# Output projection of a segment-recurrent attention in four column tiles, with the left tokens projected at the end

## The chip, the cores and the metric

The kernel runs on one core of a Trainium2 chip. The metric is the device time of one execution in microseconds (us), read as the median of several executions. PE is the matmul engine, DVE the vector engine, ACT the scalar engine, POOL the general engine, SP the engine whose queue issues most loads.

## The reference

Two branches are mixed by a gate. The second (a gated FFN) depends only on x and is done early. The first is a chain of 64 segments:

```python
for s in range(n_seg):                              # 64 segments of 32 tokens
    xs = x[:, s * seg_len:(s + 1) * seg_len, :]
    h = jnp.concatenate([mem, xs], axis=1)          # 8 memory rows + 32 rows of x, 640 wide
    q, k, v = h @ Wq, h @ Wk, h @ Wv                # 32 heads of 192 (shortened)
    p = softmax(masked(q @ k.T * scale))
    o = (p @ v) @ Wo                                # 6144 -> 640 (shortened)
    mem = o[:, :M, :]                               # 8 rows: the next segment needs them
    outs.append(o[:, M:, :])
out = g * a + (1 - g) * b
```

Everything after the first segment waits for `mem`. Four weight matrices of 7.9 MB each pass over PE in every segment. The kernel keeps most of their 84 pieces in SBUF; some 20 are loaded anew for each segment ("streamed").

## The kernel before

A segment works on 40 rows (8 memory, 32 x). For 8 of the 32 x rows, the "left tokens", Q and K are computed for all segments at the start, stored, and loaded segment by segment. The heads go in four groups ("octets"). `PROG` is the order of work in a segment:

```python
PROG = [("q", 0), ("tq", 0), ("k", 0), ("tk", 0), ("v", 0),
        ...
        ("q", 3), ("pt", 1), ("sc", 2), ("tq", 3), ("ex", 2), ("k", 3), ("pv", 1), ("tk", 3), ("v", 3),
        ("pt", 2), ("sc", 3), ("ex", 3), ("pw", 0), ("wo", 0), ("pv", 2), ("pw", 1), ("wo", 1, 0), ("pt", 3),
        ("wo", 1, 1), ("wo", 1, 2), ("pv", 3), ("wo", 2), ("wo", 3)]
```

The output projection (Wo) makes two column tiles of 64, each 320 columns wide, for all 40 rows:

```python
for h in range(2):
    ...
    fns.append(lambda e, ...: e.matmul(
        ps[64 * h:64 * h + R, OB, 0:HD], u[:, tl, cc, :], w,          # R = 40, HD = 320
        start=(c == 0), stop=(c == NCH - 1), tile_position=(0, 64 * h), skip_group_check=True))
```

The hand-over casts the result, transposes it by six small PE matmuls and copies it into the input `Hb` of the next segment:

```python
S_.add("dve", lambda e: e.tensor_copy(out=mrow[0:104], in_=ps[0:104, OB, 0:HD]), ...)
...                                                       # six (k, lo, hi, f0, h)
    fns.append(lambda e, ...: e.matmul(ps[lo:hi, bk, k * M:(k + 1) * M], mrow[:, f0:f0 + hi - lo], ident[:, 64 * h:64 * h + M], ...))
S_.add("dve", lambda e: e.tensor_copy(out=Hb[nb][:, :, 0:M], in_=ps[:, bk, 0:KT * M]...), ...)
```

The streamed pieces go through a ring of five slots. A load may start when the piece five before it is consumed:

```python
slot = stream_counter[0] % B_RING                         # B_RING = 5
S_.add("sp", lambda e, ...: e.dma_start(piece_view(key, ring_off[slot]), piece_src(key)),
       writes=[r_ring[slot]], dma_sem="ring%d" % slot, ...)
```

Of the kernel before, what the change touches and what calls it, by code (L numbers as in the profile page):

```python
# [221 lines left out]
def _build(nc, A_x, A_mem0, A_Wq, A_Wk, A_Wv, A_Wo, seg_len, w_gate, w_up, w_down,  # L222
# [9 lines left out]
    KT = Dm // 128  # L232
# [30 lines left out]
    b_scr = nc.dram_tensor("ffn_b_scratch", (S, Dm // 2 + 2), F32, kind="Internal").ap()  # L263
    xts = nc.dram_tensor("xt_scratch", (NSEG, 128, KT * L), BF, kind="Internal").ap()
    xls = nc.dram_tensor("left_xt_scratch", (NG, 128, KT * L), BF, kind="Internal").ap()
    qkl = nc.dram_tensor("left_qk_scratch", (NSEG, 128, NOCT * 2 * LW), BF, kind="Internal").ap()
# [11 lines left out]
    wsA["small"] = (96 + 2 * R + 8 + 32 + 31) // 32 * 32  # L278
# [24 lines left out]
    ffn_sz["brow"] = al(NBR * (Dm + 4) * 2)  # L303
# [4 lines left out]
    GP = 3 * HD * 2  # L308
# [38 lines left out]
    for k, n in (("stats", 0), ("maskm", 96), ("mbd", 96 + 2 * R), ("mle", 104 + 2 * R)):  # L347
        wsA_off[k] = wsA_off["small"] + n
    o_H = wsA_off["H"]
    Hb = [bview(o_H, KT * L * 2).rearrange("p (k r) -> p k r", r=L)] * 2  # L350
    r_Hm = [sreg(o_H, 8)] * 2
    r_Hxp = [sreg(o_H + 8, KT * L * 2 - 8)] * 2
# [20 lines left out]
    o_rowb, o_mrow = wsB_off["v"] + 768, wsB_off["v"]  # L373
    rowb = bview(o_rowb, HD * 2 + 4)
    rowbf = fview(o_rowb, HD * 2 + 4)
    rowbg = rowbf[:, HD // 2:HD // 2 + 1]
    r_rowb = sreg(o_rowb, HD * 2 + 4)
    mrow = bview(o_mrow, HD * 2)
    r_mrow = sreg(o_mrow, HD * 2)
# [13 lines left out]
    r_stg = [sreg(wsB_off["stg"], 256), sreg(wsB_off["stg"] + 256, NOCT * 2 * LW * 2 - 256)]  # L393
# [18 lines left out]
    o_mem0r = wsB_off["Q"] + 2 * GQ + GO  # L412
    mem0r = bview(o_mem0r, Dm * 2)
    r_mem0r = sreg(o_mem0r, Dm * 2)
# [26 lines left out]
    BW = (Dm + 4) * 2  # L441
# [19 lines left out]
    Wq2 = A_Wq.rearrange("d h e -> d (h e)").rearrange("(k p) n -> p k n", p=128)  # L461
    Wk2 = A_Wk.rearrange("d h e -> d (h e)").rearrange("(k p) n -> p k n", p=128)
    Wv2 = A_Wv.rearrange("d h e -> d (h e)").rearrange("(k p) n -> p k n", p=128)
# [13 lines left out]
    def part_src(i):  # L477
        src = piece_src(PART)
        return src[:, 1, HD:Dm] if i else src.rearrange("p c n -> p (c n)")[:, 0:GP // 2]
# [4 lines left out]
    def piece_view(key, o):  # L484
        if key[0] == 3:
# [5 lines left out]
            ("q", 2), ("pt", 0), ("sc", 1), ("tq", 2), ("ex", 1), ("k", 2), ("pv", 0), ("tk", 2), ("v", 2),  # L491
            ("q", 3), ("pt", 1), ("sc", 2), ("tq", 3), ("ex", 2), ("k", 3), ("pv", 1), ("tk", 3), ("v", 3),
            ("pt", 2), ("sc", 3), ("ex", 3), ("pw", 0), ("wo", 0), ("pv", 2), ("pw", 1), ("wo", 1, 0), ("pt", 3),
            ("wo", 1, 1), ("wo", 1, 2), ("pv", 3), ("wo", 2), ("wo", 3)]
# [37 lines left out]
    held_i = {order.index(HELD), order.index(HELD2)}  # L532
    STREAM = ((0, 0, 0), (0, 0, 4), (0, 2, 3), (0, 3, 0), (1, 0, 4), (1, 1, 0), (1, 1, 4), (1, 2, 1), (1, 3, 0), (1, 3, 3), (2, 2, 0), (2, 3, 3), (3, 0), (3, 2), (3, 6), (3, 8), (3, 11), (3, 17), (3, 20), (3, 23))
# [3 lines left out]
    assert tot_bytes - GO - GQ - sum(piece_size(key) for key in STREAM) <= res_cap  # L537
# [27 lines left out]
    part_sb = bview(o_part, GP).rearrange("p (a n) -> p a n", n=HD)  # L565
# [8 lines left out]
    def issue_ring(seg, upto):  # L574
        done = issued.get(seg, 0)
        while done <= upto:
            key = order[stream_list[done]]
            slot = stream_counter[0] % B_RING
            S_.add("sp", lambda e, slot=slot, key=key: e.dma_start(*((bview(ring_off[slot], 2 * HD), part_src(3)) if key == PART else (piece_view(key, ring_off[slot]), piece_src(key)))),
# [6 lines left out]
    def piece(seg, key):  # L586
# [5 lines left out]
        if key == HELD:  # L592
            return piece_view(key, o_held), r_held
        if key == HELD2:
            return piece_view(key, o_held2), r_held2
# [5 lines left out]
        if key == PART:  # L601
            return bview(ring_off[slot], 2 * HD), r_ring[slot]
# [14 lines left out]
    HB2 = ((5, 0, 576, 320), (6, 576, 1152, 320), (7, 1152, 1536, 640))  # L617
# [9 lines left out]

    r_heldp = [sreg(o_held + 512 * b, 512) for b in range(5)]

    def held_copy(seg, late_part):  # L630
        flat = bview(o_held, GO)
        parts = [3, 4]
        if late_part:
            nxt = [(misc[0] + 1) % 5, (misc[0] + 2) % 5]
            parts = sorted((0, 1, 2), key=lambda b: b not in nxt)
# [7 lines left out]
    left_slot = {}  # L643

# [9 lines left out]
    def left_piece(key):  # L654
        if key in res_off:
            return piece_view(key, res_off[key]), r_res[key]
        issue_left(left_stream.index(key))
        return piece_view(key, ring_off[left_slot[key]]), r_ring[left_slot[key]]
# [22 lines left out]
    for h in range(2):  # L681
        asel(maskm[64 * h:64 * h + 64], r_maskm, [[-1, R]], 0, 1, NEG)
        asel(maskm[64 * h:64 * h + 64], r_maskm, [[0, R]], -M, 1, 0.0)
# [5 lines left out]
    asel(mle, r_mle, [[8, 4], [32, 4]], 7, -1, 0.0)  # L689
    for b in range(8):  # L690
# [47 lines left out]
    def chain_init(bank):  # L738
        pv7 = psb(bank)
        S_.add("pe", [lambda e, k=k: e.transpose(pv7[:, k * M:(k + 1) * M], mem0r[0:M, k * 128:(k + 1) * 128], ident[0:M, 0:M])  # L740
                      for k in range(KT)],
               reads=[r_mem0r, r_ident], writes=[r_ps[bank]], name="mem0T")
        x_load(0)
        S_.add("act", lambda e: e.activation(out=Hb[0][:, :, 0:M], in_=pv7[:, 0:KT * M].rearrange("p (k m) -> p k m", m=M),  # L744
# [538 lines left out]
```

## Time and profile before

| | before |
|---|---|
| time, median of 3 | 1888.62 us (1880.43 to 1896.18) |
| span of the profiled execution | 1875.1 us |
| first hand-over begins | 341.0 us |
| segment, mean of 62 | 24.31 us |
| from the last hand-over to the end | 27.0 us |

In the page below, the queue lines have packets, MB and share. The group lines have the count, then busy us and mean ns, then the engine's idle time ahead of the group and what ended most of it.

```profile
q8 instruction: 272, 4.46, 0.9%
...
L949 PE MATMUL ps<-arena 128*32 128x384 bf16 x10240 | 506.0, 328 | 27.4 <-DVE arena L1179 15.8
...
L969 PE MATMUL ps<-arena 128*32 128x384 bf16 x5800 | 296.2, 329 | 21.5 <-DMA arena<-left_xt_scratch 13.7
```

To see: the passes of Q and K (L949) and V (L969) wait little; the 13.7 us ahead of V is a single wait before the first segment. The first line looks like nothing: 4.46 MB in 272 packets of 16 KB on a queue of its own. The page says PE has 34864 matmuls and as many weight loads. So 272 packets of 16384 bytes come to 272 x 16384 / 69728 = 63.9 bytes for each of these instructions, and the 320 packets of the changed kernel, with its 82018 instructions, come to 63.9 again. So by these counts q8 carries PE's own program, at 64 bytes an instruction and 256 instructions to a packet.

### The profile page before, as it was taken

How to read it: one execution, taken by the hardware profiler on the slowest of the kernel's cores; microseconds unless marked ns; L12 is line 12 of the kernel's file. 1: busy time of each engine (PE TensorE's matmuls, PEld its weight loads, DVE VectorE, ACT ScalarE, POOL GpSimd, SP SyncE). 2: the span in 40 equal slices, each digit the busy share in tenths (PEclk: the TensorE clock that was granted, in tenths of full speed). 3: DMA queues.
4: the chain of work that ended last, by engine and by line, in shares of the span. 5: the costliest groups of instructions: out<-in, count | busy, mean ns of one | idle time of the engine just before them, and what ended most of it. 6: DMA issues, size and time to landing. Idle time of an engine off the chain costs nothing.

```text
span 1875.1 us, 80690 instructions
## 1 busy us (share of the span) xinstructions
PE 1754.7 (94%) x34864; PEld 1180.5 (63%) x34864; DVE 944.5 (50%) x2960; ACT 887.6 (47%) x2093; POOL 145.0 (8%) x546
## 2 busy tenths in 40 slices
PE   8999896999999999999999999999999999999998
PEld 4556684666666666666666666666666666666665
DVE  3233243555555555555555555555555555555555
ACT  2222333555555555555444555455545555555554
POOL 1000000000000000000000000000000000000000
PEclk9999898999999999999999999999999999999999
DMA  9512657999999999999999999999999999999998
GB/s 364 218 36 83 199 154 248 300 306 305 310 305 320 305 322 306 316 299 306 302 316 299 311 301 317 295 313 304 318 299 309 310 313 317 308 300 311 314 304 271
DMA packets 281648, 536.01 MB, mean 286 GB/s; under 512 B 82114, under 2 KB 115786, under 8 KB 281290
## 3 DMA queue, kind: packets, MB, share of 16 engines
q1 hardware_dynamic: 202602, 491.34, 77.8%
q10 hardware_dynamic: 78688, 39.51, 7.6%
q8 instruction: 272, 4.46, 0.9%
q14 instruction: 86, 0.70, 0.1%
HBM read 509.62 MB, written 21.12 MB: 283 GB/s over the span
## 4 chain that ended last, share of the span: by engine, by line
PE 39%; DMA 13%; DVE 3%; ACT 2%; issue 1%; ACTq 0%; SPq 0%; DVEq 0%
PE ps L1120 12%; PE ps L949 11%; PE ps L969 7%; DMA out_dram<-arena 4%; DMA arena<-in_A_Wo_dram 3%; PE ps L1094 3%; DMA arena<-in_A_Wq_dram 3%; PE ps L1011 2%; DMA arena<-in_A_Wk_dram 1%; PE ps L1068 1%; PE ps L993 1%; PE ps L1003 1%; PE ps L1174 1%; DMA arena<-in_A_Wv_dram 1%; DVE arena L1164 1%
## 5 line engine op out<-in xcount | busy, mean ns | idle before, releaser
L949 PE MATMUL ps<-arena 128*32 128x384 bf16 x10240 | 506.0, 328 | 27.4 <-DVE arena L1179 15.8
L1120 PE MATMUL ps<-arena 128*40 128x320 bf16 x6144 | 477.4, 300 | 12.6 <-DMA arena<-in_A_Wo_dram 9.6
L1120 PEld LDWEIGHTS ps<-arena 128*40 128x40 bf16 x6144 | 317.7, 100 | 105.7 <-DMA arena<-in_A_Wo_dram 27.3
L953 ACT ACTIVATE arena<-ps 128x384 bf16<-128x384 f32 x512 | 314.6, 614 | 133.5 <-PE ps L949 89.6
L949 PEld LDWEIGHTS ps<-arena 128*32 128x32 bf16 x10240 | 253.2, 97 | 166.8 <-DVE arena L1179 20.4
L969 PE MATMUL ps<-arena 128*32 128x384 bf16 x5800 | 296.2, 329 | 21.5 <-DMA arena<-left_xt_scratch 13.7
L959 DVE STREAM_TRANSPOSE arena<-arena 128x192 f32<-128x192 f32 x512 | 190.9, 373 | 168.5 <-ACT arena L953 167.9
L969 PEld LDWEIGHTS ps<-arena 128*32 128x32 bf16 x5800 | 147.2, 97 | 111.0 <-DMA arena<-left_xt_scratch 14.1
L624 ACT ACTIVATE arena<-ps 128x576 bf16<-128x576 bf16 (+1 forms) x192 | 113.7, 592 | 213.8 <-PE ps L1120 195.2
L980 ACT ACTIVATE arena<-ps 128x384 bf16<-128x384 f32 x256 | 126.6, 495 | 180.4 <-DMA out_dram<-arena 86.6
L929 POOL COPY arena<-arena 128x96 bf16<-128x96 bf16 x256 | 68.4, 267 | 1409.9 <-PE ps L1011 780.7
L1071 DVE TENSOR_TENSOR arena<-ps,arena 128x320 bf16<-128x320 bf16 x256 | 125.7, 491 | 84.5 <-PE ps L1068 80.9
L1100 ACT ACTIVATE arena<-ps 128x320 bf16<-128x320 f32 x256 | 110.4, 431 | 91.5 <-PE ps L1094 90.8
L1094 PEld LDWEIGHTS ps<-arena 128*64 128x64 bf16 x3072 | 113.6, 125 | 56.7 <-issue 14.8
L1038 ACT ACTIVATE ps<-ps 104x160 f32<-104x160 f32 x256 | 75.5, 295 | 151.4 <-DVE ps L1028 150.8
L1094 PE MATMUL ps<-arena 128*64 128x64 bf16 (+1 forms) x3072 | 138.7, 222 | 6.8 <-ACT arena L637 2.7
L1164 DVE CAST arena<-ps 104x320 bf16<-104x320 f32 x63 | 31.0, 492 | 190.2 <-PE ps L1120 190.2
L1011 PE MATMUL ps<-arena 64*40 64x40 bf16 (+1 forms) x4096 | 120.7, 181 | 0.6 <-DVE arena L959 0.4
L892 PE MATMUL ps<-arena 128*128 128x256 bf16 x960 | 109.7, 278 | 10.1 <-ACT arena L744 5.8
L892 PEld LDWEIGHTS ps<-arena 128*128 128x128 bf16 x960 | 95.0, 100 | 24.5 <-ACT arena L744 6.1
L1026 DVE TENSOR_REDUCE arena<-ps 104x4 f32<-104x160 f32 x256 | 81.3, 318 | 51.6 <-PE ps L1011 51.2
L1011 PEld LDWEIGHTS ps<-arena 64*40 64x40 bf16 (+1 forms) x4096 | 99.9, 97 | 9.8 <-DVE arena L959 0.6
(70 smaller groups left out, 1552.7 us busy)
## 6 DMA issues: line engine op xcount, KB each, us to landing
arena<-in_A_Wk_dram SPq DMA_DIRECT2D x404, 384.0 KB, 4.8
arena<-in_A_Wo_dram SPq DMA_DIRECT2D x464, 320.0 KB, 4.5
arena<-in_A_Wq_dram SPq DMA_DIRECT2D x277, 384.0 KB, 4.7
arena<-in_A_Wv_dram SPq DMA_DIRECT2D x146, 384.0 KB, 5.3
left_qk_scratch<-arena ACTq DMA_DIRECT2D x16, 768.0 KB, 7.5
arena<-left_qk_scratch ACTq DMA_DIRECT2D x64, 192.0 KB, 5.0
arena<-in_A_Wo_dram SPq DMA_DIRECT2D x64, 80.0 KB, 3.9
ffn_b_scratch<-arena ACTq DMA_DIRECT2D x16, 161.0 KB, 2.5
```

The source lines that it names most:

```text
L624: S_.add("act", lambda e: e.activation(out=bview(o_held2, GQ)[:, c0:c1], in_=psb(b)[:, p0:p0 + c1 - c0], func=ACTF.Copy), reads=[r_ps[b]], ...
L892: S_.add("pe", [lambda e, k=k, g_=gs[k][0], i=i, bk=bk, hf=hf: e.matmul(ps[:, bk, 0:NL // 2].rearrange("p (g t) -> p g t", t=L), g_[:, i * ...
L949: S_.add("pe", [lambda e, j=j, k=k, gv=gv: e.matmul(ps[32 * j:32 * j + 32, bank, 0:384].rearrange("p (c i) -> p c i", i=32), Hb[hb][:, k, ...
L953: S_.add("act", lambda e: e.activation(out=rows_sb[m].rearrange("p (b i h) -> p b h i", b=6, h=2), in_=ps[:, bank, 0:384].rearrange("p (b ...
L959: S_.add("dve", lambda e: e.transpose(out=dst[:, :, 0:L], in_=rows_sb[m].bitcast(F32).rearrange("p (c r) -> p c r", r=L)), reads=[r_rows[m ...
L969: return [lambda e, j=j: e.matmul(ps[32 * j:32 * j + 32, bk, 0:384], lhs, g_[:, 384 * j:384 * (j + 1)], start=(k == 0), stop=(k == KT - 1) ...
L980: S_.add("act", lambda e: e.activation(out=v_sb[o % NVB], in_=ps[:, bank, 0:384], func=ACTF.Copy), reads=[r_ps[bank]], writes=[r_v[o % NVB ...
L1011: fns.append(lambda e, gp=gp, lo=lo, hi=hi, b=(3 * tl + c) // 2, h=(3 * tl + c) % 2, tl=tl, last=(c != 1): e.matmul(ps[gp:gp + R, bank, tl ...
L1071: S_.add("dve", lambda e: e.tensor_tensor(out=PTm, in0=apx(pv[:, 0:104], [[64, 2], [0, 4], [1, R]]), in1=apx(mbd, [[0, 2], [1, 4], [0, R]] ...
L1094: fns.append(lambda e, lhs=lhs, left=left, h=h, dst=dst, rhs=rhs: e.matmul(dst, lhs, rhs, start=not left, stop=left, tile_position=(0, 64 ...
L1100: S_.add("act", lambda e: e.activation(out=apx(u[:, 0, 0, :], [[R, 2], [3 * R, 4], [1, R]]), in_=ps[:, A, 0:2 * W].rearrange("p (c t r) -> ...
L1120: fns.append(lambda e, w=w, c=c, h=h, tl=tl, cc=cc, u=u: e.matmul(ps[64 * h:64 * h + R, OB, 0:HD], u[:, tl, cc, :], w, start=(c == 0), sto ...
```

## The change

Its intent is to relieve PE, the busiest engine. Wo gets four tiles of 32 rows, each 160 columns wide. To make 32 rows of the 40, the eight left tokens leave the segment's Wo. Their inputs ("left u") are stored and projected together at the end. The four Wo quarters lie in four partition groups. One DVE instruction makes the new rows (memory plus x) from them, and one DVE transpose turns them, without PE. Wo's parts move between the V passes. Stored left Q and K are loaded by octet.

```diff
-            ("q", 3), ("pt", 1), ("sc", 2), ("tq", 3), ("ex", 2), ("k", 3), ("pv", 1), ("tk", 3), ("v", 3),
-            ("pt", 2), ("sc", 3), ("ex", 3), ("pw", 0), ("wo", 0), ("pv", 2), ("pw", 1), ("wo", 1, 0), ("pt", 3),
-            ("wo", 1, 1), ("wo", 1, 2), ("pv", 3), ("wo", 2), ("wo", 3)]
+            ("q", 3), ("pt", 1), ("sc", 2), ("tq", 3), ("ex", 2), ("k", 3), ("pv", 1), ("tk", 3), ("wo", 0, 0), ("v", 2),
+            ("pt", 2), ("sc", 3), ("pw", 0), ("ex", 3), ("wo", 0, 1), ("wo", 0, 2), ("pv", 2), ("v", 3), ("pw", 1), ("pw", 2), ("wo", 1, 0), ("wo", 1, 1), ("pt", 3),
+            ("pw", 3), ("wo", 1, 2), ("wo", 2, 0), ("pv", 3), ("pw", 4), ("wo", 2, 1), ("wo", 2, 2), ("wo", 3)]
...
-                for h in range(2):
+                for j in range(4):
...
-                        ps[64 * h:64 * h + R, OB, 0:HD], u[:, tl, cc, :], w,
-                        start=(c == 0), stop=(c == NCH - 1), tile_position=(0, 64 * h), skip_group_check=True))
+                        ps[32 * j:32 * j + L, OB, 0:CB], u[:, tl, cc, 0:L], w,        # L = 32, CB = 160
+                        start=(c == 0), stop=(c == NCH - 1), tile_position=(0, 32 * j), skip_group_check=True))
...
-            S_.add("dve", lambda e: e.tensor_copy(out=mrow[0:104], in_=ps[0:104, OB, 0:HD]), ...)
-            S_.add("pe", fns, reads=[r_mrow, r_ident], writes=[r_ps[bk]], name="memT s%d" % s)
-            S_.add("dve", lambda e: e.tensor_copy(out=Hb[nb][:, :, 0:M], ...), ...)
+            S_.add("dve", lambda e: e.scalar_tensor_tensor(out=mrow, in0=ps[:, OB, 0:CB], scalar=msel, in1=xrow, op0=ALU.mult, op1=ALU.add), ...)
+            S_.add("dve", lambda e: e.transpose(out=Hb[0], in_=mrow.rearrange("p (i k) -> p k i", k=KT)), ...)
...
+    final_left()          # at the end: 384 matmuls of 128x320 for the left tokens of all segments
```

Cut: the new scratch buffers and their loads and stores, the list of streamed pieces (19 instead of 20, others, and one piece fewer in part), the masks, the contiguous stores of left Q and K on SP's queue, and the first left x taken from SBUF.

## The prediction

The sum came to 1888.6 - 166 - 15 + 63 = 1770 us. It is left as it was, but terms in it are cut below, since no trace or run had shown them: the working of step 1 (3.3 us for the new Wo; its -3.1 stays in the sum), with the figures for a matmul that it came from, and 2 us of step 7's +63 (52 + 9 are left), for a lower clock after the wait. Step 1's term: the 41 ns that a Q or K matmul of 384 columns takes in this trace would be 41 x 160 / 384 = 17.1 ns for 160 columns, 192 x 17.1 = 3.3 us, and 6.4 - 3.3 = 3.1. The 6.4 us follows from the 66.6 ns measured.

> **What bounds the kernel now.** I read the page first, then PE's timeline over two segments, then the windows, the waits and the queues.
>
> ```profile
> PE 1754.7 (94%) x34864; PEld 1180.5 (63%) x34864; DVE 944.5 (50%) x2960; ACT 887.6 (47%) x2093; POOL 145.0 (8%) x546
> DMA  9512657999999999999999999999999999999998
> L1120 PE MATMUL ps<-arena 128*40 128x320 bf16 x6144 | 477.4, 300 | 12.6 <-DMA arena<-in_A_Wo_dram 9.6
> L1164 DVE CAST arena<-ps 104x320 bf16<-104x320 f32 x63 | 31.0, 492 | 190.2 <-PE ps L1120 190.2
> q1 hardware_dynamic: 202602, 491.34, 77.8%
> q10 hardware_dynamic: 78688, 39.51, 7.6%
> ```
>
> To see: PE is busy 94% (a modelled share, ends included), and from the seventh slice on the DMA engines are nearly as full. L1120 is the output projection (Wo), 96 matmuls in each of the 64 segments. L1164 starts the hand-over of the memory to the next segment and runs 63 times between 341.0 and 1848.1 us: a segment takes (1848.1 - 341.0) / 62 = 24.3 us. Segments are 1556 us of the span, so the answer is 64 times a per-segment change, plus what happens before and after.
>
> PE's timeline over one segment's end:
>
> ```profile
> 968.77 0.49 PE L1094 MATMUL ps<-arena 128*64 128x160 bf16 x12
> 969.09 3.43 PE L1120 MATMUL ps<-arena 128*40 128x320 bf16 x48
> 973.10 0.47 PE L1174 MATMUL ps<-arena 128*128 128x8 bf16 x6 [0.58 <-DVE arena L1164]
> ```
>
> To see: 48 Wo matmuls of 320 columns need 3.43 us, less about 0.3 for the last one's own length: 47 steps of 66.6 ns. [...] 96 x 66.7 = 6.4 us a segment. After it PE stands from 972.52 to 973.86 (cast 0.49, the PE turn, a copy of 0.20): 1.34 us.
>
> Two windows, full load early and the steady state:
>
> ```profile
> 26.00:66.00 40.00, 37.97 (x303) 21.29 (x301) 11.86 (x23) 9.27 (x16) 1.28 (x4) 1.00 1.04 401
> 520.00:1870.00 1350.00, 1280.83 (x28322) 861.79 (x28322) 735.17 (x2394) 693.34 (x1671) 118.66 (x444) 1.00 0.93 308
> ```
>
> To see: clock full (1.00). The queues move 401 GB/s when only large weight rows are loaded, and 308 GB/s at a share of 0.93 in the segments. So DMA has a reserve of at most about a fifth, less with small packets. PE is the first bound, DMA close behind.
>
> [...] the gate's 80 matmuls of one column in 128x32 tiles take 0.77 us together (80.24 to 81.01), (0.77 - 0.17) / 79 = 7.6 ns apart. [...] so weight loads and issue will not limit the new Wo. [...] the Q and K passes in this trace advance 20 matmuls in 0.82 us, 41 ns[...]. [...] q1's packets average 2425 B at 77.8% x 16 x 1875 us / 202602 = 115 ns (21 B/ns); q10's small ones average 502 B at 29 ns (17 B/ns).
>
> **The change, part by part, per segment.**
> 1. Wo for 32 rows in four tiles: [...] On PE's path: -3.1.
> 2. Hand-over: cast, six PE matmuls and copy become a scalar_tensor_tensor of 128x160 and a DVE turn of 128x160. From L1185 (104x320, 547 ns) less 160 elements at the slope of the casts ((492 - 323) / 160 = 1.06 ns) I estimate 0.38; from L959 (192 elements, 373 ns) 0.34 for the turn. With hand-offs 0.85 us for 1.34: -0.5. The V pass done ahead every fourth segment now fills this gap once instead of twice, the other part moves into a V pass: no gain or loss.
> 3. x now comes in through the same scalar_tensor_tensor, so its load must have landed. It is issued after the last V pass, and that pass moves to within 3.2 us of PE work of the end (18 pairs at 0.139, one pT, one PV), perhaps 3.7 with evacuations. The old x load takes 4.2 us from issue to landing. So a new wait of about 0.5 us: +0.5.
> 4. DMA. Streamed: 12 pieces of 384 KB and 7 of 320 KB = 7.01 MB, before 7.09: no relief. Small packets: stored left Q/K by octet 512 of 384 B (before 128 of 1536 B), left u out 256, x, b and out 128 each: 1152 instead of some 384, at 29 ns / 16 engines 2.1 us instead of 0.7. At 401 GB/s the stream takes 17.5 us, with the small ones and about 0.3 of rest 19.9 us a segment. That is the floor under any PE gain.
> 5. The ring. Adding up measured PE paces, the old segment is 22.1 us of PE work against 24.3 seen (25.8 with V ahead, some 23.8 without). The new one is 18.5 without V ahead. A streamed piece may load only when the one five before it is consumed. In the old order the PE work between these lies at 4.4 to 6.5 us; landings take 4.5 to 5.3. In the new order the three pieces (3,8), (3,9), (3,11) have only 2.4 to 2.9 us. They miss by about 2 us, and as all five slots are then in a row, PE waits 2 to 3 us around Wo, where it waits about 1.6 in all today.
> Sum: 18.5 + 0.5 + about 2.5 = 21.5 without V ahead, about 22.3 with it (extra PE work of 2.4 us mostly hides waits): 21.7 on average, -2.6, x 64 = -166 us.
>
> Outside the segments:
> 6. Front. Between the left tokens' phase and segment 0 PE stands 13.7 us for the left x load, because the small-row left store occupies ACT's queue 7.12 us before it. The store becomes contiguous, on SP, and left x comes from SBUF: about -12. The memory's first transpose, which holds PE 6 us in the left phase, goes too. Sixteen DVE turns and twice the b stores come into the FFN phase, beside a DVE at a third busy: a few us. Together -15.
> 7. End. The left tokens' projection: 4 blocks x 48 x 2 = 384 matmuls of 128x320. The FFN's of this shape step at 0.136 us: 52 us, all on the path. Before it nine Wo pieces (2.95 MB, 7.4 us) and the first left u (4096 packets of 384 B, 6 to 7 us) load from the last V pass on, which ends some 4 us before Wo does: about 9 us of wait[...]. Mix and store cost what they cost today. +63.
>
> Sum: 1888.6 - 166 - 15 + 63 = 1770 us.
>
> **The rivals.** (a) *PE-bound throughout*: the ring hides everything. For it: 401 GB/s exists, and PE's waits on DMA are short today (L1120 waits 9.6 us in all). Against: the 2.4 us stretches. Segment 19.8: 1888.6 - 288 - 15 + 63 = 1650 at best; I give it little. (b) *DMA becomes the bound at the rate seen now*: engine time per segment is 0.93 x 24.3 = 22.6 us today, and the new one adds 1.4 of small packets. If this time doesn't shrink under load, a segment takes 23 to 24 and the time is 1850 to 1900. For it: the share of 0.93 at only 308 GB/s. Against: 401 GB/s at share 1.04, and single microseconds of a segment above 360. [...] (c) *A new chain of ACT waits*: the b load now waits in ACT's stream for the out store to land (landing 5.1 us), and stored left Q/K wait for the left u store. ACT is 47% busy, so about 0.5 us a segment, 30 us: 1800. (d) *The end is worse*, strided weights at the left projection halving its rate: +50, 1820.
>
> **Range and chances.** The segment is the large term: 20.8 to 22.8 us covers the mix of (a), (b) and (c), which is -224 to -96; the ends add 10 either way. That gives about 1705 to 1840. Slower or same needs (b) in full, or (b) and (d) in part: faster by over 2% (below 1850.8) 0.91, same 0.07, slower 0.02.
>
> **What would show it.** Step 1: the Wo group has 12288 matmuls of 128*32, 128x160, and an uninterrupted 48 of them last about 1 us. Step 2: DVE goes from Wo's end to Q's start in under 0.9 us. Step 3: DVE waits at the new memory rows on the x scratch, not on PE. Steps 4 and 5: DMA share 0.95 or more, 330 to 350 GB/s in the segments, PE waits on Wo loads up from 9.6 to 60 us or more. Step 6: the 13.7 us wait is gone. Step 7: 384 matmuls at 0.136 after the last segment, and a tail of some 60 us. I am wrong if the segment is over 23 us (DMA), under 20.5 us (no ring loss), or the tail is over 80 us.

## The result

The changed kernel takes 1946.99 us, the median of four executions (1941.83 to 1955.31). The kernel before took 1885.07 us in its four (1880.43 to 1896.18). The ratio is 1.0324, with a 95% interval from 1.0261 to 1.0386: 3% slower. A ratio in this document is the mean time of one kernel's fast runs over that of the other's of the same rounds, so it is not quite the ratio of the medians quoted. Executions over 1.5% slower than the fastest of the same kernel are left out of the means.

The spans split at the first and the last of the 63 hand-overs:

| part | before | after | difference |
|---|---|---|---|
| up to the first hand-over | 341.0 us | 318.8 us | -22.2 |
| 62 segments | 1507.1 us (24.31 each) | 1527.3 us (24.63 each) | +20.2 |
| from the last hand-over to the end | 27.0 us | 94.0 us | +67.0 |
| span | 1875.1 us | 1940.1 us | +65.0 |

So both ends came out much as predicted (-15 and +63), and the segments, which should have given back 166 us, took 20 us more.

The page of the changed kernel, the line of engines and that of the instruction queue:

```profile
PE 1678.7 (87%) x41009; PEld 1124.4 (58%) x41009; DVE 944.5 (49%) x2988; ACT 939.3 (48%) x2220; POOL 300.6 (15%) x795
...
q8 instruction: 320, 5.24, 1.1%
```

To see: PE has 41009 matmuls for 34864, because four narrow tiles need twice as many instructions as two wide ones. It has 76 us less of busy time, and is idle for more. The queue has 48 more packets.

The window over most of the segments (us, then busy time and count of PE, PEld, DVE, ACT and POOL, then granted clock, DMA share, GB/s):

```profile
520.00:1845.00 1325.00, 1136.06 (x32234) 744.38 (x32238) 701.39 (x2315) 713.56 (x1722) 248.65 (x646) 0.98 0.92 306
```

To see: the data rate did not rise (306 GB/s, 308 before), the share of the DMA engines fell to 0.92, and the granted clock is 0.98 for 1.00.

The groups of the changed kernel, with up to three releasers each:

```profile
L1018 PE MATMUL ps<-arena 128*32 128x384 bf16 x10240 | 527.7, 330 | 92.7 <-DVE arena L1251 46.5 <-DMA arena<-in_A_Wq_dram 20.5 <-ACT arena L640 10.5
...
L1196 PE MATMUL ps<-arena 128*32 128x160 bf16 x12288 | 337.2, 243 | 127.7 <-DMA arena<-in_A_Wo_dram 98.5 <-issue 17.6 <-DMA arena<-left_u_scratch 9.7
...
L1249 DVE SCALAR_TENSOR_TENSOR arena<-ps,arena 128x160 bf16<-128x160 f32 x63 | 24.2, 384 | 100.3 <-PE ps L1196 97.7 <-DMA arena<-x_segment_scratch 2.6
...
L1251 DVE STREAM_TRANSPOSE arena<-arena 128x160 bf16<-128x160 bf16 x63 | 22.5, 357 | 2.2
```

To see: Wo (L1196) waits 98.5 us for its weights where the old one waited 9.6, and 17.6 us with the releaser "issue", which means that the profile shows nothing that it waited for. The hand-over (L1249, L1251) takes 384 + 357 ns, as estimated.

PE over one segment's end (start us, length us, work, and in brackets the idle time before it):

```profile
1005.19 0.32 PE L1196 MATMUL ps<-arena 128*32 128x160 bf16 x8 [0.93 <-DMA arena<-in_A_Wo_dram]
1005.79 0.32 PE L1196 MATMUL ps<-arena 128*32 128x160 bf16 x8 [0.28 <-DMA arena<-in_A_Wo_dram]
...
1007.59 1.42 PE L1196 MATMUL ps<-arena 128*32 128x160 bf16 x70
1010.09 0.38 PE L1196 MATMUL ps<-arena 128*32 128x160 bf16 x10 [1.08 <-issue]
1011.45 2.60 PE L1018 MATMUL ps<-arena 128*32 128x384 bf16 x40 [0.97 <-DVE arena L1251]
1013.82 1.50 PE L1038 MATMUL ps<-arena 128*32 128x384 bf16 x16
```

To see: three kinds of loss in 9 us. Eight matmuls at a time wait for a streamed piece of Wo. Then 70 Wo matmuls run in 1.42 us, (1.42 - 0.23) / 69 = 17.2 ns apart with about 0.23 us taken off for the last one's own length. That is the pace which step 1's 3.3 us needs (3.3 us / 192 = 17.2 ns), and then PE stands 1.08 us for no shown reason. After the hand-over the 40 matmuls of Q and K need 2.60 us instead of the 1.81 that the same 40 need elsewhere: the trace records half clock (a granted clock of 0.50) from 1012.32 to 1015.73 us. In the segments (from the eleventh hand-over on) there are 17 such stretches, sixteen of 3.41 us and one of 6.83, which is 1.18 us to a segment; before there was one.

The tail:

```profile
1867.70 1.56 PE L1196 MATMUL ps<-arena 128*32 128x160 bf16 x79
1878.93 0.32 PE L1196 MATMUL ps<-arena 128*32 128x160 bf16 x1 [9.67 <-DMA arena<-left_u_scratch]
1881.36 54.68 PE L1329 MATMUL ps<-arena 128*128 128x320 bf16 x384 [2.11 <-DMA arena<-left_u_scratch]
```

To see: the left tokens' projection takes 54.68 us (52 predicted), behind 9.67 + 2.11 us of waiting for their input (about 9 predicted). The granted clock is 0.50 up to 1886.12 us, where the matmuls step 268 ns; after it they step 136 ns. The 2 us from step 7's term stood for this.

### The profile page after: what moved, and what is told of

Same layout as the page of the kernel before. It is cut to its first block, busy times and chain, and to the rows that moved or that the text cites. A ratio compares the mean times of both kernels' runs of the same rounds, so it can differ in the third digit from the quotient of the medians.

```text
span 1940.1 us, 93507 instructions
## 1 busy us (share of the span) xinstructions
PE 1678.7 (87%) x41009; PEld 1124.4 (58%) x41009; DVE 944.5 (49%) x2988; ACT 939.3 (48%) x2220; POOL 300.6 (15%) x795
## 4 chain that ended last, share of the span: by engine, by line
PE 61%; DMA 32%; issue 3%; DVE 3%; SPq 1%; POOL 0%; DVEq 0%; ACT 0%; POOLq 0%; ACTq 0%
PE ps L1018 17%; DMA arena<-in_A_Wo_dram 17%; PE ps L1196 10%; DMA arena<-in_A_Wq_dram 9%; PE ps L1038 8%; PE ps L952 5%; PE ps L1164 3%; PE ps L1329 3%; PE ps L835 3%; PE ps L838 3%; DMA arena<-in_A_Wv_dram 3%; PE ps L1082 3%; PE ps L1074 2%; PE ps L853 1%; PE ps L856 1%
## 5 line engine op out<-in xcount | busy, mean ns | idle before, releaser
L1018 PE MATMUL ps<-arena 128*32 128x384 bf16 x10240 | 527.7, 330 | 92.7 <-DVE arena L1251 46.5
L1196 PE MATMUL ps<-arena 128*32 128x160 bf16 x12288 | 337.2, 243 | 127.7 <-DMA arena<-in_A_Wo_dram 98.5
L1018 PEld LDWEIGHTS ps<-arena 128*32 128x32 bf16 x10240 | 246.0, 97 | 257.4 <-DVE arena L1251 62.1
L1196 PEld LDWEIGHTS ps<-arena 128*32 128x32 bf16 x12288 | 226.8, 100 | 202.8 <-DMA arena<-in_A_Wo_dram 139.5
L1038 PE MATMUL ps<-arena 128*32 128x384 bf16 x6100 | 308.6, 332 | 11.8 <-issue 7.5
L1183 POOL COPY arena<-arena 128x96 bf16<-128x96 bf16 x256 | 159.2, 622 | 659.8 <-DVE arena L1177 438.6
L1038 PEld LDWEIGHTS ps<-arena 128*32 128x32 bf16 x6100 | 157.8, 98 | 103.3 <-issue 16.3
L640 ACT ACTIVATE arena<-ps 128x384 bf16<-128x384 bf16 (+2 forms) x192 | 114.0, 594 | 117.2 <-POOL arena L1000 81.4
L998 POOL COPY arena<-arena 128x96 bf16<-128x96 bf16 x256 | 68.4, 267 | 615.9 <-PE ps L1082 461.5
L1164 PE MATMUL ps<-arena 128*64 128x160 bf16 (+1 forms) x3072 | 139.0, 226 | 3.0 <-issue 2.6
L1164 PEld LDWEIGHTS ps<-arena 128*64 128x64 bf16 x3072 | 103.2, 126 | 61.7 <-DVE arena L1095 22.6
L666 ACT ACTIVATE arena<-ps 128x256 bf16<-128x256 bf16 x320 | 102.0, 387 | 16.9 <-PE ps L1196 7.6
L952 PE MATMUL ps<-arena 128*128 128x256 bf16 x960 | 105.1, 273 | 1.8 <-DVE arena L963 1.8
```

The costliest lines, as they stand in the source:

```text
L640: S_.add("act", lambda e: e.activation(out=bview(o_held2, GQ)[:, c0:c1], in_=psb(b)[:, p0:p0 + c1 - c0], func=ACTF.Copy), reads=[r_ps[b]], ...
L952: S_.add("pe", [lambda e, k=k, g_=gs[k][0], i=i, bk=bk, hf=hf: e.matmul(ps[:, bk, 0:NL // 2].rearrange("p (g t) -> p g t", t=L), g_[:, i * ...
L1018: S_.add("pe", [lambda e, j=j, k=k, gv=gv: e.matmul(ps[32 * j:32 * j + 32, bank, 0:384].rearrange("p (c i) -> p c i", i=32), Hb[hb][:, k, ...
L1038: return [lambda e, j=j: e.matmul(ps[32 * j:32 * j + 32, bk, 0:384], lhs, g_[:, 384 * j:384 * (j + 1)], start=(k == 0), stop=(k == KT - 1) ...
L1164: fns.append(lambda e, lhs=lhs, left=left, h=h, dst=dst, rhs=rhs: e.matmul(dst, lhs, rhs, start=not left, stop=left, tile_position=(0, 64 ...
L1183: S_.add("pool", lambda e: e.tensor_copy(out=dst, in_=u.rearrange("p t c r -> p (t c) r")[:, :, L:R]), reads=[r_uT[o % NUB]], writes=r_ul[ ...
```

## The experiments

Four theories were to be told apart. The **ring**: Wo's loads start too late, since in the new order five streamed pieces follow each other closely. The **data rate**: the DMA engines give no more than some 310 GB/s with these transfers. The **row order** of Wq, Wk and Wv in DRAM, which the change altered, costs data rate. And, formed after the first four runs, the **fetch**: PE runs out of instructions, since Wo in four tiles uses them up faster than q8 brings them. In the texts L is the ring, B the data rate and F the fetch. A piece is "aliased" below when two pieces of a weight share one place in SBUF. This makes room, and the result is wrong.

A segment's time is the mean distance of the hand-overs. Waits per segment are sums over the segments from the eleventh hand-over on.

**e1, changed kernel with a ring of eight** (three V pieces aliased; wrong).

```diff
-    B_RING = int(opts.get("ring", 5))
+    B_RING = int(opts.get("ring", 8))
+    ALIAS = {(2, 0, 1): (2, 0, 0), (2, 0, 3): (2, 0, 2), (2, 1, 1): (2, 1, 0)}
```

> The changed kernel with eight ring slots instead of five; three resident V pieces share the place of three others to make room, so the result is wrong on purpose; the streamed bytes are the same. Theory L (the load loop: five slots, each refilled only when PE has used it, and about 5 us from issue to landing): deeper slots let the queues run towards the 401 GB/s of the pure load, the segment falls from 24.6 us to about 21 us and the time to about 1720 us, DMA at 345 GB/s or more in the segments. Theory B (bandwidth: some 305 GB/s is all that the queues give beside the engines at work): the segment stays within 0.3 us of 24.6, landings grow from 5 to 7 or 8 us, time 1930 to 1950 us.

Measured: 1975.99 us, ratio 1.0459 (1.034 to 1.058), segment 25.09 us. The waits for weights are gone from PE, and the kernel is slower than with them. The stands marked "issue" grew to 1.63 us a segment at Wo alone, half clock to 2.63 us. So the ring is not the whole cause; neither of the two expectations for this run came. PE's timeline between two of these stands:

```profile
1036.68 0.52 PE L1200 MATMUL ps<-arena 128*32 128x160 bf16 x18
1039.33 0.45 PE L1200 MATMUL ps<-arena 128*32 128x160 bf16 x14 [2.12 <-issue]
1039.71 0.53 PE L1168 MATMUL ps<-arena 128*64 128x160 bf16 x12
1040.17 1.00 PE L1042 MATMUL ps<-arena 128*32 128x384 bf16 x20
1041.00 0.73 PE L1200 MATMUL ps<-arena 128*32 128x160 bf16 x32
1041.65 0.28 PE L1141 MATMUL ps<-arena 104*64 104x104 bf16 x4
1041.87 1.06 PE L1200 MATMUL ps<-arena 128*32 128x160 bf16 x32
1042.86 0.53 PE L1168 MATMUL ps<-arena 128*64 128x160 bf16 x12
1043.32 1.59 PE L1200 MATMUL ps<-arena 128*32 128x160 bf16 x80
1046.08 1.81 PE L1022 MATMUL ps<-arena 128*32 128x384 bf16 x40 [1.17 <-DVE arena L1255]
1047.72 0.65 PE L1042 MATMUL ps<-arena 128*32 128x384 bf16 x10
1050.38 0.67 PE L1042 MATMUL ps<-arena 128*32 128x384 bf16 x10 [2.01 <-issue]
```

To see, and to add up: from 1039.33 to just before 1050.38 there are 14 + 12 + 20 + 32 + 4 + 32 + 12 + 80 + 40 + 10 = 256 matmuls. With a weight load each that is 512 instructions, exactly two packets. q8's packets start at 1036.99, 1041.08 and 1048.08 us and take 0.9 to 1.1 us each. The stands end 1.3 and 1.4 us after the first and the third of them have landed. So the place of a stand is fixed by the count of instructions, not by what the instructions do.

**e2, kernel before with a ring of eight** (same aliases; wrong).

```diff
-    B_RING = int(opts.get("ring", 5))
+    B_RING = int(opts.get("ring", 8))               # and the same ALIAS
```

> The kernel before with the same eight slots (wrong result on purpose). Theory L: it was already held by the loop, so it gains too, but only down to its PE work of 22 to 23 us a segment: 24.3 to about 23, time 1800 to 1830 us. Theory B: unchanged, 1870 to 1890 us. If it was bound by PE and only the changed kernel is bound by loads: unchanged here, and e1 gains.

Measured: 1848.25 us, ratio 0.9783 (0.972 to 0.984), segment 23.83 us at 314 GB/s. The old kernel does gain 0.5 us a segment from the ring, the changed one doesn't (the interval of the ratio lies below 1 and reaches across the 2% line).

**e3, changed kernel with 9 streamed pieces instead of 19** (ten aliased).

```diff
-    STREAM = ((0, 1, 1), (0, 2, 1), (0, 3, 1), (0, 3, 3), ...            # 19 pieces
+    STREAM = ((0, 2, 1), (0, 3, 3), (1, 0, 3), (1, 1, 4), (1, 3, 4), (2, 2, 4), (3, 3), (3, 6), (3, 9))
+    ALIAS = {(0, 1, 1): (0, 1, 0), ...}                                  # the other ten
```

> The changed kernel with 9 streamed pieces instead of 19; the other ten read a resident piece instead (wrong result on purpose). Both theories of loads: the segment falls to PE's own work with its dependences, my sum being 18.5 us without and 21 us with left V, so about 19.5 to 20.5 us on average and a time of 1620 to 1690 us. A theory that the new order of work has waits of its own between the engines (ACT's DMA waits, the memory hand-over): it stays above 22 us, over 1780 us.

Measured: 1729.67 us, ratio 0.9155, segment 21.48 us at 179 GB/s. PE is marked idle 1.33 us a segment, so its work is about 20.2 us. PE waits for no weight load in the segments here. The segment lies between the two expectations (19.5 to 20.5, over 22): the loads cost much, and something besides them is dearer than predicted. Taking the ten pieces out of the stream gives 24.63 - 21.48 = 3.15 us a segment.

**e4, the old row order of Wq, Wk and Wv** (wrong).

```diff
-    Wq2 = A_Wq.rearrange("d h e -> d (h e)").rearrange("(p k) n -> p k n", p=128)
+    Wq2 = A_Wq.rearrange("d h e -> d (h e)").rearrange("(k p) n -> p k n", p=128)      # Wk2, Wv2 alike
```

> The changed kernel with the rows of Wq, Wk and Wv taken as before, so that neighbouring partitions read neighbouring rows 12 KB apart rather than 60 KB apart (wrong result on purpose). A theory that the new row order makes the loads slower in HBM: the segment falls by 1 us or more, time under 1890 us. Theories L and B: no difference, within 10 us of 1945 us.

Measured: 1961.49 us, ratio 1.0382, segment 24.98 us. No gain: the row order is not the cause. (The two ratios, 1.0382 and 1.0324, lie within each other's intervals.)

**e5, half of Wo's instructions; e6, the same with a ring of eight and the aliases of e1** (two of the four column tiles left out; wrong).

```diff
-                for j in range(4):
+                for j in range(2):
```

> New theory F, after e1: PE's instructions come by DMA too (queue q8's 16 KB packets number exactly PE's records times 64 B: 272 before, 320 after), four-tile Wo eats 256 instructions in some 2.2 us, and beside the weight loads a packet does not come that fast; PE then stands with nothing but issue named, and goes to half clock. This kernel leaves out two of the four column tiles of every segment's Wo (wrong on purpose): the same 3.3 us of PE work (two tiles of 160 columns side by side), the same loads, half of Wo's instructions, back to about the number of before. F: the waits named issue at Wo fall from about 1 us a segment to under 0.2, half clock too; with five slots the loads still hold PE, segment 23 to 24 us, time 1850 to 1910 us. Theories of the loads alone (L, B): no change, 1930 to 1960 us.

Measured for e5: 1920.48 us, ratio 1.0198, segment 24.15 us. The stands for instructions fell to 0.08 us a segment, but the waits for Wo's loads stayed at 1.66 us: they take the place of what was removed. So in the changed kernel as it stands, the instructions alone are worth 24.63 - 24.15 = 0.48 us a segment.

> The same with eight ring slots (as e1). F with L: both limits are gone, the segment falls from 25.1 us (e1) to 21 to 22 us, DMA at 335 GB/s or more, time 1720 to 1790 us, and clock back to 0.99. B (305 GB/s is the ceiling): stays at 24.5 us and 1930 us or more.

Measured for e6: 1893.89 us, ratio 1.0057, segment 23.93 us at 314 GB/s. With both gone a third wait appears: DVE waits at the hand-over for x. From the issue of the x load to Wo's end there are 3.77 us, and the load takes 5.56 us, so the hand-over begins 1.9 us after Wo's end. This is step 3 of the prediction, 3.7 us of work against the load, hidden until then.

**e7, kernel before with each Wo matmul cut into two of 160 columns**, in two column tiles. This doubles the instructions of Wo at the same array work. Its result is off by a relative error of 0.101, which was not intended.

```diff
-                        ps[64 * h:64 * h + R, OB, 0:HD], u[:, tl, cc, :], w,
+                    for y in range(2):
+                            ps[64 * h:64 * h + R, OB, HD // 2 * y:HD // 2 * y + HD // 2], u[:, tl, cc, :], w[:, HD // 2 * y:HD // 2 * y + HD // 2],
```

> The kernel before with each Wo matmul of 320 columns cut into two of 160 in the same column tile: as many Wo instructions as the changed kernel, at the old rate of array work (6.4 us), right result. If the number of instructions as such (more bytes to fetch, 0.6 packets a segment) is what costs: slower by 2% or more, 1925 us or up. F as a matter of rate (256 instructions now take 4.3 us, not 2.2): within 15 us of before, hardly any issue waits.

Measured: 1914.3 us, ratio 1.0165 (1.010 to 1.023), segment 24.90 us for 24.31. The median lies between the two expectations: more than a loss within 15 us, less than 2%, though the interval reaches past 2%. Here an instruction pair should take half of the old 66.6 ns, 33 ns (an estimate; with the steps measured below it is 6.7 us / 192 = 35 ns). That is slower than the 25 ns a pair at which the closest packets of any run land (below), and still PE stood 0.29 us a segment for instructions. The cut itself also made the steps between Wo's matmuls 6.7 us a segment for 6.2. (The diff leaves out that the four matmuls of a pass were also reordered.) So this run shows the cost of more instructions at a slower pace only roughly.

**e8, another order and another choice of streamed pieces**, which spreads Wo and the streamed loads more evenly (correct).

```diff
-            ("q", 3), ("pt", 1), ("sc", 2), ... ("tk", 3), ("wo", 0, 0), ("v", 2),
+            ("q", 3), ("wo", 0, 0), ("pt", 1), ("sc", 2), ... ("wo", 0, 1), ("k", 3), ("wo", 0, 2), ("pv", 1), ("tk", 3), ("v", 2), ("wo", 1, 0),
```

> A version meant to be better, right result: the changed kernel with Wo's parts spread further (a third of an octet's Wo between Q, K and V passes from pass q3 on) and another choice of 12 + 7 streamed pieces, so that five pieces on from any one there are at least 5.3 us. F with L: fewer waits on Wo loads (1.6 us to under 0.7) and on issue, segment 22.5 to 23.5 us, time 1810 to 1880 us. B: unchanged, 1930 us or more.

Measured: 1972.7 us in the one fast run (the other, 2006.87 us, counts as slow, so there is no ratio), segment 25.07 us. The waits for Wo's loads went, but waits for Wk's loads (0.77 us) and for the evacuations ahead of the early Wo (nearly 1 us) came. Not a remedy.

**e9, half of Wo, ring of eight, and x loaded early into a buffer of its own**, so that all three waits are nearly away at once (wrong). **e10, the same with the whole Wo.** Four V pieces are aliased in both.

```diff
-    xrow = bview(o_H, CB * 2)
+    xrow = bview(wsA_off["xrow"], CB * 2)            # no longer shares its place with H
-        if o == NOCT - 1 and s + 1 < NSEG:
-            x_load(s + 1)                            # now after the third K pass
```

> e6 showed a third wait: the x load, issued after the last V pass, lands 5.6 us later and the hand-over stands for it 1.9 us, after which PE runs half of the next pass at half clock. Here (e6 plus) x has a buffer of its own and is loaded during pass k2, eight microseconds or more ahead (wrong result on purpose). If these three latencies (ring, instructions, x) are what holds the segment: period 23.9 to 21 to 22 us, DMA at 340 GB/s or more, low clock under 0.5 us a segment, time 1740 to 1790 us. If some 310 GB/s is a ceiling of the queues (B): the period stays at 23.5 us or more and the wait turns up elsewhere, 1870 us or more.

Measured for e9: 1778.25 us, ratio 0.9431, segment 22.1 us. The queues moved 340 GB/s at a share of 0.97, and no stretch of the segments ran at half clock. The window over most of the segments (columns as above):

```profile
520.00:1600.00 1080.00, 983.23 (x24607) 673.79 (x24596) 638.11 (x2103) 642.90 (x1563) 227.54 (x588) 1.00 0.97 340
```

To see: the theory that some 310 GB/s is all falls. But at 340 GB/s the share is 0.97, so e9 itself may be near what the engines give with these packets, which is not shown; no run has more in the segments.

> The same with all of Wo's instructions (e1 plus an early x). Then only the instruction fetch is left as a limit of the three. F: issue waits stay at some 2 us a segment and the period is 23 to 24 us, 1850 to 1900 us. If the half clock in e1 came from the hand-over and not from the fetch: 22 us, 1790 us.

Measured for e10: 1971.74 us, ratio 1.0458, segment 25.11 us at 300 GB/s. That is slower than either expectation. The other half of Wo costs 3.0 us a segment, though it runs beside the first half: the steps between Wo's matmuls take 3.6 us a segment here and 3.1 in e9.

**e13, e9 with the missing half put back as matmuls of one column**: the full count of instructions, where the added 96 matmuls a segment would take 0.7 us at the 7.6 ns of the gate's matmuls (an estimate).

```diff
-                        ps[32 * j:32 * j + L, OB, 0:CB], u[:, tl, cc, 0:L], w,
+                        ps[32 * j:32 * j + L, OB, 0:CB if j < 2 else 1], u[:, tl, cc, 0:L], w[:, 0:CB if j < 2 else 1],
```

> e9 with the left-out half of Wo's matmuls put back as matmuls of a single column (wrong on purpose): the instruction count of the full four-tile Wo, but hardly more array work than e9 (96 matmuls at some 8 ns, 0.7 us a segment). If instructions to fetch are what parts e9 (22.1 us a segment) from e10 (25.1): 24 us or more with 1 to 2 us of issue waits, clock under 0.97, time 1890 us or more. If it is the array work, PSUM writes or power of four full tiles: 22.2 to 23.0 us and 1780 to 1840 us.

Measured: 1975.27 us, ratio 1.0477, segment 25.38 us for e9's 22.1. The Wo group of e9:

```profile
L1200 PE MATMUL ps<-arena 128*32 128x160 bf16 x6144 | 280.0, 234 | 15.0 <-DMA arena<-left_u_scratch 8.7 <-DVE arena L1147 2.7 <-issue 0.5
```

and of e13:

```profile
L1200 PE MATMUL ps<-arena 128*32 128x1 bf16 (+1 forms) x12288 | 295.4, 204 | 125.7 <-issue 110.6 <-DMA arena<-left_u_scratch 11.1 <-DVE arena L1147 2.3
```

To see: the same useful work with 6144 matmuls more, nearly empty ones, and "issue" goes from 0.5 to 110.6 us. The steps between Wo's matmuls are 3.4 us a segment for 3.1. This run decides: once ring and x are out of the way, what costs is the number of instructions.

**e14, e10 with some of Wo's thirds moved earlier and apart**, so that 112 instead of 144 of Wo's 192 matmuls stand after the last V pass. The last 80 still stand almost in a row.

```diff
-            ("q", 3), ("pt", 1), ("sc", 2), ... ("k", 3), ("pv", 1), ("tk", 3), ("wo", 0, 0), ("v", 2),
+            ("q", 3), ("wo", 0, 0), ("pt", 1), ("sc", 2), ... ("k", 3), ("wo", 0, 1), ("pv", 1), ("tk", 3), ("v", 2), ("wo", 0, 2),
```

> e10 (eight slots, early x, all of Wo) with thirds of an octet's Wo moved earlier, between the passes from q3 on, so that 112 instead of 144 of Wo's 192 matmuls stand after the last V pass (wrong only through the shared resident pieces). If the fetch is a matter of how densely short instructions stand: issue waits fall from 2.6 us a segment to about 1, period 23 to 24 us, 1840 to 1900 us. If of the total only: as e10, 1960 us or more.

Measured: 1983.57 us, ratio 1.0521, segment 25.21 us. This much spreading did not help: 1.34 us of stands for instructions stayed at Wo, and 0.9 us of waits for evacuations came.

**e11, changed kernel with only the list of streamed pieces chosen more evenly** (correct).

```diff
-    STREAM = ((0, 1, 1), (0, 2, 1), (0, 3, 1), (0, 3, 3), ... (3, 5), (3, 6), (3, 8), (3, 9), (3, 11), (3, 21))
+    STREAM = ((0, 0, 3), (0, 1, 0), (0, 1, 3), (0, 2, 0), ... (3, 2), (3, 5), (3, 9), (3, 12), (3, 17), (3, 21))
```

> The changed kernel, right result, with nothing changed but which 12 + 7 pieces are streamed: chosen so that five pieces on there are at least 5.1 us of PE work, where the changed kernel's own list has 2.4 us in the worst place. If the clustered list is what makes PE wait 1.6 us a segment on Wo loads: waits on loads under 0.8, the period 23.6 to 24.1 us, 1880 to 1910 us. If not (the place of the wait only moves, as e8 suggests): within 15 us of 1945 us or slower.

Measured: 1919.68 us, ratio 1.0181 (1.008 to 1.028), segment 24.13 us. The wait for Wo's loads fell from 1.57 to 0.26 us a segment. Of these 1.3 us only 0.5 were gained: the stands for instructions at Wo grew from 0.31 to 0.71 us, waits for Wk's loads to 0.73. The waits behaved as expected, the time lies just outside the 1880 to 1910 us.

**e12, kernel before with 10 streamed pieces instead of 20** (aliased; wrong).

```diff
-    STREAM = ((0, 0, 0), (0, 0, 4), (0, 2, 3), (0, 3, 0), ...            # 20 pieces
+    STREAM = ((0, 0, 0), (0, 3, 0), (1, 1, 4), (1, 3, 3), (2, 3, 3), (3, 0), (3, 6), (3, 11), (3, 20), (3, 23))
+    ALIAS = {(0, 0, 4): (0, 0, 3), ...}                                  # the other ten
```

> The kernel before with ten of its 20 streamed pieces replaced by resident ones (wrong result on purpose), to see what its PE order costs without load waits. If it was bound by PE as I read it: the period falls by less than 1 us, from 24.3 to 23.3 us or above, time 1815 to 1850 us. If it was bound by loads: 22.5 us or less, under 1775 us.

Measured: 1821.72 us, ratio 0.9662, segment 23.43 us. The loads of these ten pieces cost the old kernel only 24.31 - 23.43 = 0.88 us a segment, and PE waits for no weight load in the segments that are left.

**e15, kernel before with the start of the changed one** (first left x from SBUF, first left Q and K loaded ahead of the last store; correct, five rounds). **e16, the same with a ring of six and one more streamed piece** in the room that the sixth slot takes (correct, five rounds).

```diff
+            if o_ == NOCT - 1 and hf:
+                held_put(HELD, ...)
+                stg_load(0)
+                S_.add("pool", lambda e: e.tensor_copy(out=Hx..., in_=XL_flat[:, 0:KT * L]), ...)
-    xleft_load(0)
-    stg_load(0)
```

and for e16 besides:

```diff
-    B_RING = int(opts.get("ring", 5))
+    B_RING = int(opts.get("ring", 6))
-    STREAM = ((0, 0, 0), (0, 0, 4), (0, 2, 3), ...
+    STREAM = ((0, 0, 0), (0, 0, 4), (0, 1, 2), (0, 2, 3), ...
```

> A version meant to be better, right result: the kernel before, whose only change is the start of the chain: the first left x comes from SBUF by GpSimd, and the first stored left Q and K are asked for ahead of the last left stores. The 13.7 us stand of PE before segment 0 goes, and with it a stretch of half clock: 12 to 16 us, ratio 0.992 to 0.994 of before. Segment period unchanged at 24.3 us.

Measured for e15: 1894.41 us, ratio 1.0044 (1.002 to 1.007). The gain of the start did not come. PE's timeline before the first segment, in the kernel before:

```profile
299.82 0.34 PE L969 MATMUL ps<-arena 128*32 128x384 bf16 x4
313.90 3.01 PE L969 MATMUL ps<-arena 128*32 128x384 bf16 x36 [13.74 <-DMA arena<-left_xt_scratch]
```

and in e15:

```profile
320.55 0.66 PE L952 MATMUL ps<-arena 128*32 128x384 bf16 x12
330.75 0.83 PE L952 MATMUL ps<-arena 128*32 128x384 bf16 x8 [9.54 <-DMA arena<-in_A_Wq_dram]
```

To see: the 13.74 us wait is gone (in the kernel before, the trace records half clock from 303.07 to 316.72 us, within and after it), and a wait of 9.54 us for the first streamed pieces begins 21 us later than it did. Their loads were issued only from 323.70 us on, behind 13 loads of Wo pieces in the same queue. The changed kernel issues the ring ahead of that; e15 did not take this part over. The first hand-over came at 350.5 us for 341.0, so this one wait, shorter than the old one, does not explain the whole loss; 1.90 and 3.59 us of new waits stand between the two lines shown.

> The same with six ring slots, paid for by one more streamed piece (21), right result. If deeper slots help as in e2 more than 393 KB more a segment cost: period 24.0 us and ratio under 0.985. If the extra bytes eat it: 24.3 to 24.8 us, 1870 to 1900 us.

Measured for e16: 1878.27 us, ratio 0.9967 (0.995 to 0.998), segment 24.27 us, 0.3% faster than the kernel before. It is the fastest correct kernel of the study, but by less than the 2% that would count.

### The count that settles the fetch

The trace has the landing of each q8 packet and the start of each PE instruction. From these one can keep a stock: 449, plus 256 for each packet landed, less the instructions started. 449 is one constant for all kernels, set so that the lowest stock of the changed kernel is 0; with it the lowest stock of every kernel that stands often is 0 as well. The table has, from the eleventh hand-over to the last, the stock just before a packet lands, and PE's stands of over 0.3 us marked "issue":

| kernel | instruction packets | stock before landing: lowest / 5% / median | stands | of these with one packet's stock at their end | us a segment |
|---|---|---|---|---|---|
| before | 207 | 30 / 68 / 136 | 0 | | 0 |
| e12, before, few streams | 207 | 121 / 143 / 183 | 0 | | 0 |
| after | 244 | 0 / 4 / 92 | 40 | 40 | 0.69 |
| e3, after, few streams | 244 | 0 / 33 / 141 | 27 | 27 | 0.39 |
| e5, half Wo | 205 | 0 / 42 / 126 | 5 | 5 | 0.08 |
| e1, ring of eight | 244 | 0 / 0 / 84 | 86 | 86 | 2.38 |
| e9, half Wo, ring of eight, x early | 205 | 0 / 7 / 71 | 36 | 36 | 0.57 |
| e13, e9 with empty matmuls | 244 | 0 / 0 / 88 | 86 | 86 | 2.90 |

Over all 18 traces there are 620 such stands, and every one ends with a stock of 255 or 256: by this count PE has used up all that was fetched, and goes on with the first instruction of the packet that has just come, 1.1 to 1.7 us after it landed. Four more readings of the same count:

- The stock before a landing never exceeds 280. So by this count PE never holds more than 280 + 256 = 536 instructions, little more than two packets.
- No two packets land closer than 3.25 us in any run, also at 179 GB/s. That is 12.7 ns an instruction, 25 ns for a matmul with its weight load, and it is the best case: where the stock had run out (two or less, 278 landings in all runs), the packet came 6.2 us after the one before it in the median, and 4.5 us at the least. Wo in two tiles of 320 uses a pair in 66.6 ns and the Q and K passes in 41 (before), Wo in four tiles in 17.2 (after).
- With fewer streamed weights the stock is higher in the median at the same count of instruction packets (183 for 136 in e12, 141 for 92 in e3). So in these runs the packets come earlier with fewer weight loads. By which way is not shown.
- A packet's own transfer takes 0.95 to 1.02 us in the median of each run, in light and in loaded runs alike. Where the rest of the 3.25 us goes is not shown by any run.

## Why the prediction was wrong

The direction was wrong (slower had been given a chance of 0.02), and two steps failed. The first is the inference from the gate's 80 matmuls that "weight loads and issue will not limit the new Wo". The 80 do run 7.6 ns apart. But they are 160 instructions, less than one packet's 256, so that burst says nothing about a pace that must be kept up. With ring and x out of the way, the supply of instructions alone holds the segment at 25.1 us (e10) and 25.4 us (e13), against 22.1 us without it (e9). One page line of the kernel before (q8) had the supply to be read.

The second is step 5's sum of paces, 18.5 us for the new segment. It is too small even where no weight load is waited for: e3 takes 21.03 us in the same kind of segment, and only 0.39 us of the difference are stands for instructions. That the first step is not the whole miss is seen in e5: nearly without stands for instructions, and with the changed kernel's ring and x, a segment still takes 24.15 us where the prediction had 21.7.

The sizes follow from the two runs with few streamed pieces. Some 10 pieces are still streamed in both, but PE waits for none of them in the segments. The prediction's figures are for a segment without left V ahead, so the table takes three segments of four. The fourth, with left V ahead, took 25.76 us before and 25.74 after. In us:

| | streamed as it is | few streams | cost of the other ten pieces |
|---|---|---|---|
| measured, before | 23.84 | 22.85 (e12) | 0.99 |
| measured, after | 24.28 | 21.03 (e3) | 3.25 |
| gain | -0.44 | 1.82 | |
| predicted, before | 23.8 | 22.1 | 1.7 |
| predicted, after | 21.5 | 18.5 | 3.0 |
| gain | 2.3 | 3.6 | |

So of the 2.74 us by which the gain was missed, 1.8 are missing on PE itself, 0.7 were taken for waits of the old kernel that did not exist, and 0.25 is the new cost of streaming. The second table takes PE's time apart, start to start of its matmuls, in us a segment, all four kinds of segment averaged:

| | before | e12 | e3 | after |
|---|---|---|---|---|
| idle, as the profile marks it | 1.20 | 0.77 | 1.31 | 3.47 |
| steps within Wo | 6.22 | 6.15 | 3.40 | 4.08 |
| steps within other kinds | 12.46 | 12.13 | 12.30 | 12.54 |
| steps from one kind to another | 4.41 | 4.41 | 4.56 | 4.56 |

- **Step 1** (Wo, -3.1): right where Wo runs, 6.15 to 3.40 is -2.75 with few streams. With full streams it is -2.14, and the waits that came with it (Wo's loads 1.57, instructions) make it nothing. Part of the gain is lost where PE goes into Wo and out of it: ten such steps a segment in both kernels, 0.88 us together in e12 and 1.41 in e3 (counted in the last row of the table). The prediction had no term for this.
- **Step 2** (hand-over, -0.5): right in its instructions, 384 and 357 ns for the estimated 380 and 340. PE stands 0.97 us there in the timeline shown where it stood 1.34; from Wo's end to Q's start it is 1.04 us in the mean for 1.57. But idle time as a whole grew by 0.54 us even from e12 to e3, 0.39 of it stands for instructions. Steps 1 and 2 together were to give 3.6 and gave 1.82.
- **Step 3** (wait for x, +0.5): right in mechanism, hidden in the changed kernel (DVE waited 2.6 us for it in all). It shows as soon as ring and fetch are relieved (e6).
- **Step 4** (floor of 19.9 us from DMA): never reached, and so not tested. The rate stayed at 306 GB/s while PE stood; the most that any run shows in the segments is e9's 340, where the floor took 401.
- **Step 5** (the ring, 2 to 3 us of waits for 1.6 today): the new cost is near, 3.25 for 3.0 with step 3, but partly by luck: waits for weights are 1.95 us a segment (2 to 3 predicted), the wait for x 0.05 (0.5 predicted), and the rest is half clock and more stands for instructions. The old cost is wrong: PE waited 0.25 us a segment for weights, and all its idle time was 1.20 us, less than the 1.6 named. There the prediction took the whole distance between its sum of paces, 22.1, and the time seen for waits that the change would replace. The sum itself was too small, by 0.75 us before and, with what the fetch adds, by 2.5 us after.
- **Step 6** (front, -15): -22.2. The 13.7 us wait is gone.
- **Step 7** (end, +63): +67.0; the wait came to 11.8 us for 9 and the projection to 54.68 for 52, half clock included.

The range has a slip of its own: -96 us in the segments and +10 at the ends give 1888.6 - 96 - 15 + 63 + 10 = 1851 us at the top, not 1840. It changes nothing here.

Within the cost of streaming three limits overlap: the ring, the fetch, and behind them the load of x. Taking one away changes the segment by -0.5 (half of Wo's instructions, e5), +0.5 (ring, e1) or -0.5 (even list, e11), because the next one takes over. Only with all three nearly away (e9, where 0.57 us of stands for instructions remain) does it fall to 22.1 us, and putting back nothing but instructions (e13) brings 25.4. That is why the mechanism was hard to see in the trace of the changed kernel, where the waits for Wo's loads are the longest line.

Half clock adds to it: 1.18 us a segment after the change, 2.63 in e1, 3.29 in e13, none in e9, 0.07 before. In the changed kernel's tail the left tokens' matmuls step 268 ns at a granted clock of 0.50 and 136 ns at 1.00, so at that ratio half clock costs at most half of it, 0.6 us in the changed kernel (an estimate). It comes after stands of PE; in the timeline above, PE stood 1.08 + 0.97 = 2.05 us of the 3.41 us before the clock fell. That the stands cause it is argued from this and not tested by itself. It can follow other stands too: e6 had 2.42 us of half clock with hardly any stand for instructions, and waits of 1.9 us at the hand-over.

Of the rivals, (b), the data rate of today, named 1850 to 1900 and so came nearest with its number, but its reason does not hold. (a) was far off. (c) left little: ACT as the releaser of Q and K makes 10.5 us in all. (d) was right in sign and small, 54.68 us for 52, and not by its reason: at full clock the left tokens' matmuls step 136 ns, as the FFN's do.

What stays open: why a packet of instructions takes at least 3.25 us from the one before it, why the steps into and out of Wo grew, and whether an order of work exists that keeps four tiles within the supply. The two orders tried here (e8, e14) do not; both still end with a run of Wo (48 and 80 matmuls).

## What to carry to other kernels

Count instructions as a stream with a rate of its own. Divide the matmuls and loads of the fastest burst by its length and set that against the packets of the instruction queue (here a pair each 17.2 ns against one each 25 ns at best); a burst shorter than the stock (here 160 instructions) proves nothing about a long one. When tiles are split further, count the instructions too: here Wo's steps fell from 6.15 to 3.40 us (e12, e3) while its matmuls went from 96 to 192 a segment. And a gap between a sum of paces and the measured time is not a wait for loads until a run with fewer loads has shown it.
